# A decode step (gated attention plus GLU): written engine order, and wo split by heads around the last V pair

## The chip, the cores and the metric

One core of a Trainium2 chip. The metric is the device time of one execution in microseconds (us), lower is better. Each set of runs was made on one chip, and sets fell on different chips. The kernel before ran in the rounds of each set, but set 3 was compared with the eleven executions of before from set 2 (same chip) and only two new ones. An execution is called fast when it lies within 1.5% of the fastest of its kernel in the set, slow otherwise. "Span" is the time from the first to the last instruction of a profiled execution.

## The reference, cut to what matters

```python
g = sigmoid((x * gate_w).sum())                       # one number
q = x @ wq                                            # 32 heads of 128
k, v = last W = 4096 rows of the caches, 8 kv heads   # 4 query heads each
a = softmax(q k^T / sqrt(128)) v   @ wo               # wo: 4096 x 512
b = (sigmoid(x @ w_gate) * (x @ w_up)) @ w_down       # 512 -> 1792 -> 512
out = g * a + (1 - g) * b                             # 512 numbers, one token
```

One token, so each weight and each cache row is used once: 30.7 MB are read, in this order of use: wq 4.2 MB, K 8.4, w_gate and w_up 3.7, V 8.4, w_down 1.8, wo 4.2.

## The kernel before

The K and V caches come in four pairs of kv heads (2.1 MB each). VectorE transposes each K half pair (kT), TensorE forms scores S, a softmax over all heads follows, then PV, then a head selection (o_ps), a small transpose (oX, oY), and the products with wo row block by row block (`add_row`: two matmuls of 128x256 for a block of 128 rows). The GLU branch adds its 14 row blocks of w_down to the same sum a_ps. The engines' order is left to a scheduler, which may move instructions within what their data allow.

```python
# loads, all on one queue, in this order
wq; K0..K3; w_gate; w_up (7/8 at once, the last 1/8 in four loads "wx" of 32 rows)
V0, V1, V2; V3 first half; w_down[0:7]; V3 second half; w_down[7:14]
wo in pieces of 8, 8, 8, 5, 2, 1 row blocks                   # waits for wq's buffer
...
S_ps = ps_S.tile([P, 4, 512], F32)                            # scores of all, one tile
for v in range(2):                                            # softmax
    nc.scalar.activation(e_sb[:, v], S_ps[...], AF.Exp, ...)
    nc.vector.transpose(eT[...], e_sb[:, v])                  # L242
...
nc.vector.tensor_scalar_add(sge, sge, 1.0)                    # GLU's gate
nc.vector.reciprocal(sg, sge)                                 # L266
nc.vector.scalar_tensor_tensor(h_sb, gu_ps[1], gg[:, 1:2], sg, ...)   # L268
nc.vector.transpose(hT, h_sb)                                 # L273
...
for a in range(4):                                            # PV, L304
    for m in range(16):
        if a == 3 and m == 8: down(0, 7)
        nc.tensor.matmul(pv_ps[32*a:32*a+32], lhsT=eT[:, a, 4*m:4*m+4], rhs=vv[a][:, 4*m:4*m+4], ...)
nc.scalar.copy(pv_sb, pv_ps)                                  # all heads at once
down(7, 10); o_ps (4 matmuls); oT; down(10, 12); oX; oY_ps; oY; down(12, 14)
for c in range(32):                                           # wo behind everything
    add_row(oY[:, c:c+1], wo_sb[:, c], ...)                   # L290
res; store
```

## Time and profile before

| | before |
|---|---|
| time, median of the first set | 84.41 us (84.08 to 84.76, 4 runs) |
| time, median of all 35 runs of the later sets | 83.8 us (82.85 to 85.02) |
| profiled execution | 83.79 us, span 81.6 us |
| loads end (the DMA engines' busy share falls to 0.07) | 75.2 us, the last packet at 75.5 |
| scores | 27.6 to 44.1 us |
| PV begins | 57.8 us |
| last matmul ends | 78.87 us |

How to read it: what a change can win is what lies between the end of the loads and the end of the span. The lines that this rests on are in the prediction.

### The profile page before, as it was taken

To read this page: it belongs to the slowest core of one execution; us is meant where nothing else is said; L and a number is where in the kernel's file an instruction comes from. 1 tells how busy PE (TensorE), PEld (TensorE's weight loads), DVE (VectorE), ACT (ScalarE), POOL (GpSimd) and SP (SyncE) were. 2 spreads that over 40 slices of the span, in tenths; PEclk is the share of its full clock that TensorE was granted. 3 is DMA by queue.
4 is the path that set the end of the run, shared out by engine and by line. 5 is a ranking of instruction groups with operands and counts; after the bars stand their busy time and mean duration, and the time that the engine had idled before them with its cause. 6 is when DMAs were issued, how large, how long until landed. Compare 5 with 4: busy or idle time off the path is not lost.

```text
span 81.6 us, 791 instructions
## 1 busy us (share of the span) xinstructions
PE 51.6 (63%) x313; PEld 24.0 (29%) x313; DVE 38.6 (47%) x50; ACT 10.1 (12%) x18; POOL 3.3 (4%) x10
## 2 busy tenths in 40 slices
PE   0200286999400499999999063300999999967960
PEld 0200122344000233444443033000433444545830
DVE  0601820034999999999903995699300000002020
ACT  2300000376500000000000200910000000020010
POOL 7800000000000000000000000000000000000000
PEclk9999999999998555999999997555555999999999
DMA  5969969999999999999999999999999999995000
GB/s 161 353 289 482 514 273 490 393 418 474 401 426 458 410 434 425 436 422 412 421 422 458 410 426 450 409 426 391 417 428 420 420 422 422 424 399 217 0 0 1
DMA packets 3050, 30.71 MB, mean 376 GB/s; under 512 B 356, under 2 KB 616, under 8 KB 1128
## 3 DMA queue, kind: packets, MB, share of 16 engines
q1 hardware_dynamic: 3042, 30.67, 89.7%
q8 instruction: 2, 0.03, 0.2%
q10 hardware_dynamic: 6, 0.00, 0.0%
HBM read 30.67 MB, written 0.00 MB: 376 GB/s over the span
## 4 chain that ended last, share of the span: by engine, by line
PE 55%; DVE 24%; DMA 15%; ACT 1%; issue 1%
PE S_ps L215 20%; PE pv_ps L304 17%; DMA wq_sb<-in_A_wq_dram 15%; PE q_ps L184 8%; PE a_ps L290 6%; DVE kT L209 5%; DVE sg L266 4%; DVE pm L222 3%; DVE eT L242 3%; DVE h_sb L268 3%; DVE qbig L197 2%; DVE qtT L189 2%; PE o_ps L313 1%; PE gu_ps L255 1%; DVE hT L273 1%
## 5 line engine op out<-in xcount | busy, mean ns | idle before, releaser
L215 PE MATMUL S_ps<-kT,qbig 128*128 128x512 bf16 x64 | 16.6, 424 | 6.2 <-DVE qbig L197 6.2
L209 DVE STREAM_TRANSPOSE kT<-kn 128x2048 f32<-128x2048 f32 x8 | 17.8, 2275 | 0.0
L304 PE MATMUL pv_ps<-vv,eT 128*32 128x512 bf16 x64 | 14.2, 436 | 0.0
L215 PEld LDWEIGHTS <-qbig 128*128 128x128 bf16 x64 | 6.7, 106 | 16.1 <-DVE qbig L197 7.0
L184 PE MATMUL q_ps<-wq_sb,xT 128*128 128x512 bf16 x32 | 8.4, 428 | 1.0 <-DMA wq_sb<-in_A_wq_dram 1.0
L304 PEld LDWEIGHTS <-eT 128*32 128x32 bf16 x64 | 5.8, 109 | 7.6 <-issue 3.6
L315 DVE TENSOR_TENSOR oT<-o_ps,rb 128x32 bf16<-128x32 f32 x1 | 0.2, 191 | 15.2 <-PE o_ps L313 15.2
L189 DVE STREAM_TRANSPOSE qtT<-q_sb 128x512 f32<-128x512 f32 x4 | 2.8, 702 | 7.5 <-ACT q_sb L186 7.5
L203 PE MATMUL S_ps<-ident,other 2*128 2x512 bf16 x4 | 2.0, 611 | 5.8 <-DVE other L141 5.8
L186 ACT CAST q_sb<-q_ps 128x512 bf16<-128x512 f32 x8 | 4.7, 585 | 6.5 <-PE q_ps L184 6.5
L184 PEld LDWEIGHTS <-xT 128*128 128x128 bf16 x32 | 3.4, 108 | 6.4 <-issue 3.7
L279 PE MATMUL rb_ps<-lsel,ones_f 128*128 128x32 f32 x2 | 0.6, 398 | 5.6 <-DVE lsel L277 5.6
L222 DVE TENSOR_REDUCE pm<-S_ps 128x1 f32<-128x1024 f32 x2 | 2.4, 1219 | 3.2 <-PE S_ps L215 3.2
L290 PE MATMUL a_ps<-wo_sb,oY 128*1 128x256 bf16 x64 | 3.7, 272 | 0.0
L263 ACT ACTIVATE sge<-gu_ps 128x448 f32<-128x448 f32 x1 | 0.5, 543 | 23.1 <-PE gu_ps L258 23.1
L290 PEld LDWEIGHTS <-oY 128*1 128x1 bf16 x64 | 2.8, 84 | 0.7
L266 DVE RECIPROCAL sg<-sge 128x448 f32<-128x448 f32 x1 | 3.0, 2954 | 0.0
L309 ACT COPY pv_sb<-pv_ps 128x512 f32<-128x512 f32 x1 | 0.6, 586 | 18.7 <-PE pv_ps L304 18.7
L268 DVE SCALAR_TENSOR_TENSOR h_sb<-gu_ps,gg,sg 128x448 bf16<-128x448 f32 x1 | 2.2, 2154 | 1.5 <-PE gu_ps L255 1.5
L166 DVE TENSOR_TENSOR gpr<-xr 1x512 f32<-1x512 bf16 x1 | 0.7, 679 | 4.6 <-DMA xr<-in_gate_w_dram 4.6
L149 PE MATMUL xt_ps<-ident,xr 1*128 1x1 bf16 x4 | 0.3, 166 | 3.5 <-POOL ident L130 3.5
L203 PEld LDWEIGHTS <-other 2*128 2x128 bf16 x4 | 0.6, 158 | 6.2 <-DVE other L141 5.9
(60 smaller groups left out, 32.5 us busy)
## 6 DMA issues: line engine op xcount, KB each, us to landing
kn<-in_A_k_cache_dram SPq DMA_DIRECT2D x4, 2048.0 KB, 27.2
vv<-in_A_v_cache_dram SPq DMA_DIRECT2D x3, 2048.0 KB, 19.1
wq_sb<-in_A_wq_dram SPq DMA_DIRECT2D x1, 4096.0 KB
wo_sb<-in_A_wo_dram SPq DMA_DIRECT2D x3, 1024.0 KB, 22.9
vv<-in_A_v_cache_dram SPq DMA_DIRECT2D x2, 1024.0 KB
wg_sb<-in_B_w_gate_dram SPq DMA_DIRECT2D x1, 1792.0 KB, 32.9
wd_sb<-in_B_w_down_dram SPq DMA_DIRECT2D x2, 896.0 KB
wu_sb<-in_B_w_up_dram SPq DMA_DIRECT2D x1, 1568.0 KB
```

Of the source, the lines that this page charges most:

```text
L184: nc.tensor.matmul(q_ps[:], lhsT=xT[:, c:c + 1].to_broadcast([P, P]), rhs=wq_sb[:, c, ks], start=(c == 0), stop=(c == DC - 1))
L186: nc.scalar.copy(q_sb[:, ks], q_ps[:])
L189: nc.vector.transpose(qtT[:].bitcast(F32)[:, kq], q_sb[:].bitcast(F32)[:, kq])
L203: nc.tensor.matmul(S_ps[:, u, :], lhsT=other[:].rearrange("p o y u -> p (o y u)"), rhs=ident[0:2, 0:2].rearrange("p (o y) -> p o y", o=1). ...
L209: nc.vector.transpose(kT[:].bitcast(F32), kn[a][:, v * KB:(v + 1) * KB, :] .rearrange("p n d -> p (n d)").bitcast(F32))
L215: nc.tensor.matmul(S_ps[:, 2 * v + hb, :], lhsT=q_st[:, a, dhi, :, t], rhs=k_v[:, hb * 16:(hb + 1) * 16, dhi, :, t], start=False, stop=(a ...
L222: nc.vector.tensor_reduce(pm2[:, v:v + 1], S_ps[:, 2 * v:2 * v + 2, :].rearrange("p a b -> p (a b)"), axis=AX.X, op=ALU.max)
L242: nc.vector.transpose(eT[:, :, v * KB:(v + 1) * KB, :].rearrange("p a n r -> p n a r"), e_sb[:, v, :].rearrange("p (n a r) -> p n a r", a= ...
L266: nc.vector.reciprocal(sg[:], sge[:])
L268: nc.vector.scalar_tensor_tensor(h_sb[:].rearrange("p j i -> p i j"), gu_ps[1][:, 0:FQ].rearrange("p (i j) -> p i j", j=NJ), gg[:, 1:2], s ...
L290: nc.tensor.matmul(a_ps[32 * i:32 * i + 1, i, 0:HN], lhsT=lhsT, rhs=rhs[:, i * HN:(i + 1) * HN], start=start, stop=stop)
L304: nc.tensor.matmul(pv_ps[32 * a:32 * a + 32, :, :], lhsT=eT[:, a, 4 * m:4 * m + 4, :].rearrange("p n r -> p (n r)"), rhs=vv[a][:, 4 * m:4 ...
```

## The change

Four things at once. Its intent: nothing but the last pieces of the last load shall remain to do once the stream of loads is over.

1. From the query projection on, TensorE, VectorE and ScalarE run in the order in which the program is written (`manual_schedule`), and that order puts GLU's vector work behind the exponentials' transposes and the first K transpose between the query's.
2. S becomes two tiles (one for each half v), so that the first maximum needn't wait for the second half; PV takes one of their PSUM buffers and a_ps the other.
3. Heads in two halves: the first half's selection, transpose and wo rows run while V3 is awaited. wo is stored by halves of heads, one loaded before V3, one after.
4. w_down moves to the end, in pieces of 8, 3, 2 and 1 row blocks.

```diff
+    WD_SPLIT = (0, 8, 11, 13, 14)
+    ORDERED = {PE, DVE, Activation}
-    ps_S = tile_pool(name="ps_S", bufs=1, space=PSUM)
+    ps_S = tile_pool(name="ps_S", bufs=2, space=PSUM)
 ... loads
-            load_pair(vv[3], A_v_cache, 3, 0, NP // 2)
-            dq.dma_start(wd_sb[:, 0:7], wd_v[:, 0:7])
-            load_pair(vv[3], A_v_cache, 3, NP // 2, NP)
-            dq.dma_start(wd_sb[:, 7:14], wd_v[:, 7:14])
-    for c0, c1 in zip(WO_SPLIT[:-1], WO_SPLIT[1:]):
-        dq.dma_start(wo_sb[:, c0:c1, :], wo_v[:, c0:c1, :])
+            dq.dma_start(wo_sb[:, 0], wo_v[0])
+            load_pair(vv[3], A_v_cache, 3, 0, NP // 2)
+            load_pair(vv[3], A_v_cache, 3, NP // 2, NP)
+            dq.dma_start(wo_sb[:, 1], wo_v[1])
+    for j0, j1 in zip(WD_SPLIT[:-1], WD_SPLIT[1:]):
+        dq.dma_start(wd_sb[:, j0:j1, :], wd_v[:, j0:j1, :])
 ... front
+    ctx.enter_context(tc.manual_schedule(engines=ORDERED))
+        if k == 1: kTs[0, 0] = k_transpose(0, 0)          # in the query loop
+            copy = nc.scalar.copy if qd == 3 else nc.vector.tensor_copy   # 2 of 8 qbig copies
 ... GLU's sge, sg, h_sb, hT now written behind eT, rs, lsel
 ... tail
+    pv(0)
+    (rb_ps matmul, rb)
+    pv(1); pv_copy(0); pv(2)
+    heads_out(0); heads_rows(0)
+    pv(3); pv_copy(1)
+    out_rows(0, 0, 8);  heads_out(1)
+    out_rows(0, 8, 16); heads_rows(1)
+    out_rows(1, 0, 16)
+    for j in range(NJ): add_row(hT[:, j, 0:1], wd_sb[:, j, :], False, j == NJ - 1)
```

## The prediction

> **What bounds the kernel now.** I read the page's slices first, then the waits of the DMA queue, then the chain of work that ended last, then the timeline of the softmax stage and of the tail.
>
> The slices (2.04 us each; the busy tenths of TensorE, VectorE, the granted clock and the DMA engines):
>
> ```profile
> PE   0200286999400499999999063300999999967960
> DVE  0601820034999999999903995699300000002020
> PEclk9999999999998555999999997555555999999999
> DMA  5969969999999999999999999999999999995000
> ```
>
> The DMA row stands at 9 from slice 6 to 35. So the 30.7 MB of inputs arrive without a break, at about 0.42 MB per us, until 75 us, and the kernel can't end before that. But the span is 81.6 us: for the last three slices nothing is loaded and TensorE works alone. That tail is what can be won. The PE row has two holes, near 23 us and from 45 to 57 us, and after each the clock row says 5: half clock.
>
> When each load lands can be read from the SyncE queue, whose issues each wait for the load eight places before:
>
> ```profile
> 46.74 0.33 SPq L124 DMA_DIRECT2D wo_sb<-in_A_wo_dram  x1
> 51.63 0.33 SPq L124 DMA_DIRECT2D wo_sb<-in_A_wo_dram  x1
> 56.54 2.80 SPq L124 DMA_DIRECT2D wo_sb<-in_A_wo_dram  x2
> 61.20 0.33 SPq L124 DMA_DIRECT2D wo_sb<-in_A_wo_dram  x1
> ```
>
> The releasers are V0, V1 and V2, and at the last line the first w_down half: the V pairs of 2.1 MB land at 46.74, 51.63 and 56.54 us, one each 4.9 us, so 0.426 MB/us. After 61.20 us 6.16 MB are still to come; at this rate they end at 75.7 us. The row of DMA by stretches agrees: full rate to 74 us, half rate to 75.2, nothing after.
>
> The end of the chain:
>
> ```profile
> 54.58 2.25 DVE eT L242 x2
> ...
> 57.91 11.63 PE pv_ps L304 x52
> ...
> 70.20 1.83 PE pv_ps L304 x8
> 72.03 0.02 issue
> 72.05 0.59 ACT pv_sb L309
> 72.65 0.04 issue
> 72.69 1.09 PE o_ps L313 x8
> ...
> 74.47 4.40 PE a_ps L290 x78
> 78.87 0.40 DVE res L330
> ```
>
> The whole attention output must pass eviction, head selection and a transpose before the first wo row may be multiplied, and all 64 wo matmuls (of the 78) come after it, although most of wo lay there long before. PV itself begins at 57.9 us, 11 us after V0 landed, because the exponentials' transposes stand behind the GLU on VectorE:
>
> ```profile
> 46.85 2.95 DVE L266 RECIPROCAL sg<-sge 128x448 f32<-128x448 f32 x1
> 51.75 2.15 DVE L268 SCALAR_TENSOR_TENSOR h_sb<-gu_ps,gg,sg 128x448 bf16<-128x448 f32 x1 [1.53 <-PE gu_ps L255]
> 53.94 0.65 DVE L273 STREAM_TRANSPOSE hT<-h_sb 128x448 bf16<-128x448 bf16 x1
> 54.51 2.33 DVE L242 STREAM_TRANSPOSE eT<-e_sb 128x1024 bf16<-128x1024 bf16 x2
> ```
>
> **What the Trainium skill says.** "TensorE: Matmul & The Clock Gate", Part 1, says that the clock is 1.2 or 2.4 GHz, set by activity in free-running windows of 3413 ns. The trace agrees on the windows: the clock falls at 25.96 and 49.85 us and rises at 32.8 and 63.5 us, all whole multiples of 3.41 us apart, and 512-column matmuls stand 427 ns apart before such a rise and 215 ns after. The page speaks of an idle window; here the window 46.44 to 49.85 us had 1.43 us of matmuls and the clock still fell, while 1.97 us in the window before it kept the clock. So I put the threshold at about half a window. "DMA: Bandwidth & Descriptors", Where 436 GB/s comes from, gives a fabric ceiling of 435 GB/s; the 426 measured here lie close to it, so I expect no order of loads to end the stream sooner. The same page, Anatomy of one DMA, says that completion follows the last byte by a write receipt; the 0.4 us between the last busy DMA (75.2) and my 75.7 is my allowance.
>
> **The change part by part.**
>
> Start of the scores. Before, VectorE did the first two K transposes and the last query transpose in such an order that the eight qbig copies ended at 27.6. Now the first K transpose follows the first query transpose: kn0 lands at 17.8 (the third wx issue, which waits for it), so it takes 17.8 to 20.1 (2.27 us), the query transposes go on to 22.65 (the last cast ends at 21.95, plus 0.7), six copies stay on VectorE (6 of 8 of 1.77, 1.3 us), two go beside them to ScalarE. Scores begin at about 24.0 instead of 27.56. Then seven transposes follow at 2.21 us (13.28 for 6), to 39.4; TensorE needs only 8 x 0.215 = 1.72 us for each, and ends about 41.3 instead of 44.1: 2.8 us earlier.
>
> Softmax. The first maximum (1.2 us) now runs before the last scores end, as S is two tiles. From 41.3: maximum 1.2, to 42.55; pm and mt to 43.15; from there the old durations of hm, mb, nb and exp (49.72 to 52.20) give the first eT at 45.7, two of 1.15, to 48.0. The 2.95 + 2.15 + 0.65 + 0.38 = 6.1 us of GLU are now behind it and end at about 54.5, where nobody waits. PV can begin at 47 to 48 instead of 57.8. This is ten us, but **it is not worth ten us**: V0 has only just landed (46.74). PV is from now on paced by the loads.
>
> Loads. The same bytes in another order after V2 (56.54): first half of wo 61.5, V3 in halves 63.9 and 66.4, second half of wo 71.3, w_down's 8, 3, 2 and 1 blocks 73.7, 74.7, 75.3 and about 75.7 us (estimates: bytes over 0.426). V3 lands 2.6 us later than now, but the work behind it shrinks. The buffers allow the order: wo takes the one that wq left at 21 us; the queue's eight places are never empty.
>
> TensorE from there, at full clock: pv(2) 56.6 to 60.1; first half's heads 1.1 for o_ps, 0.45 on VectorE, 0.3 for oY, to 62; pv(3) from 63.9 in two parts of 8 x 0.215, ends 68.3; ScalarE copy 0.6; 16 of the first half's 32 row matmuls beside it (16 x 0.0565 = 0.9; rate from 78 in 4.40); o_ps 69.0 to 70.1; oT and oX 0.45 with the other 16 rows beside; oY at 71.5. That is just when the second half of wo lands (71.3). Its 32 rows take 1.8, to 73.4; then the w_down rows follow their pieces; after the last piece (75.7) 2 matmuls remain, with latency 0.35: **76.05 us against 78.87**. The end (res, the store, 2.75 us from 78.87 to 81.6) doesn't change. Gain 2.8 us: about 81.7 us.
>
> Added: four matmuls for two oY (one before), two evictions of 64 rows for one of 128, some 0.6 us more of small work, all under a load's wait except the second half's, which is in the sum.
>
> **Rivals.**
>
> 1. The clock falls in front of V3. Between 61.95 and 63.9 us TensorE has nothing to do, and little between 65.65 and 66.35. A window that ends between about 63.3 and 65.6 us holds 0.85 to 1.5 us of matmuls, as little as the one at 46.44 or less. For it: that is two thirds of all positions of the free-running window. Against: the page wants an idle window, and one full window (3.4 us) of half-clock matmuls raises it again, as at 63.5 in the trace. Cost, worked for three positions: falling at 64.5, pv(3) ends at 69.0 and nothing is lost, since oY (71.9) then wants only 0.6 us more and the rows catch up before the last piece; falling at 63.5 without the next window counting, or at 65.4, pv(3) ends near 70, oY comes at 73.7 to 74.1, and 60 rows of 0.0565 follow: 77.3 to 77.5. Time 82.9 to 83.1 us, a gain of only 1.6 to 1.9%.
>
> 2. The load stream hides nothing more, and all of the gain is lost: the tail at half clock throughout. 60 rows at 0.113 instead of 0.0565 cost 3.4 us more, TensorE ends at 79, no gain: 84.5 us. Against: the rows kept the clock in the trace before from 70 to 79 us. I give it 5%.
>
> 3. The small last pieces (1 to 3 KB runs) stretch the stream. The stream before ended in pieces of the same kind (5, 2 and 1 KB runs) and had half rate for its last 1.2 us, so I count the same once more. If it were 1 us longer: 82.7 us.
>
> 4. The early gain counts in full (PV 10 us sooner, end at 72 us). The loads speak against it: not before 75.7.
>
> **Range and chances.** Half for the case bound by loads (81.7), four tenths for the clock's fall (81.9 to 83.1), one tenth for something unseen. Executions before spread over 0.7 us. My number is 82.1 us, range 81.2 to 83.4. The line of 2% faster is 82.8 us: the load case lies a full 1 us beyond it, about half of the clock cases lie beyond it. Faster 0.68, same 0.30, slower 0.02.
>
> **What would show it.** Right: scores begin near 24 and end near 41.3; PV begins between 46.8 and 48.5; GLU's reciprocal after eT; TensorE's waits in front of pv for V, not for eT; V3 landing at 66.4; the last w_down matmul at 76 us within 0.5 us of its load; span 78.8. The clock row with a 5 near 64 to 70 us would be rival 1: then oY comes after 73 us, and the w_down rows don't wait. Wrong: a DMA row with gaps after slice 13, a last landing later than 76.3, or a new wait on VectorE (rb or oT behind the GLU after 60 us).

## The result, and the profile after

The first set gave 80.98 us (80.8 to 81.74, 4 runs) against 84.41 (84.08 to 84.76): ratio 0.961, 95% interval 0.954 to 0.968. Ratios here are the mean time of one kernel's fast runs over that of the other's in the same rounds, so not quite the ratio of the medians quoted; as far as I can reproduce them, the profiled executions of the later sets are left out. Faster, as forecast, but 80.98 lies below the range of 81.2 to 83.4.

The slices of the kernel after (2.0 us each), TensorE, VectorE, granted clock and DMA:

```profile
PE   0200193999914788998887557999789579998940
...
DVE  0600820029859999999986349999300200001020
PEclk9999999999999999999999995699999985899997
DMA  3979998999999999999999999999999999999600
```

The DMA row has no gap, as before, and now TensorE works until just behind it: the idle hole of TensorE from 45 to 57 us is gone, and the tail of three slices without loads is down to two. The chain that ended last, in order of time, is no longer TensorE's (in the kernel before, S, PV and the rows of a_ps were 43% of it) but the stream's:

```profile
32.68 18.96 DMA vv<-in_A_v_cache_dram
51.64 0.02 issue
51.66 24.14 DMA wd_sb<-in_B_w_down_dram
75.79 0.04 issue
75.84 0.65 PE a_ps L306 x6
76.48 0.40 DVE res L366
```

VectorE's timeline in the softmax stage shows the new order, eT ahead of GLU:

```profile
46.73 2.37 DVE L280 STREAM_TRANSPOSE eT<-e_sb 128x1024 bf16<-128x1024 bf16 x2 [1.91 <-ACT e_sb L278]
...
49.75 2.95 DVE L290 RECIPROCAL sg<-sge 128x448 f32<-128x448 f32 x1
52.82 2.17 DVE L292 SCALAR_TENSOR_TENSOR h_sb<-gu_ps,gg,sg 128x448 bf16<-128x448 f32 x1
```

TensorE's timeline at the end (start, duration, line, what; in brackets the idle time before and what ended it):

```profile
63.96 4.65 PE L319 MATMUL pv_ps<-vv,eT 128*32 128x512 bf16 x13 [0.90 <-DMA vv<-in_A_v_cache_dram]
...
72.50 1.91 PE L306 MATMUL a_ps<-wo_sb,oY 128*1 128x256 bf16 x32 [0.27 <-DVE oY L339]
74.25 1.41 PE L306 MATMUL a_ps<-wd_sb,hT 128*1 128x256 bf16 x22
75.84 0.60 PE L306 MATMUL a_ps<-wd_sb,hT 128*1 128x256 bf16 x6 [0.18 <-DMA wd_sb<-in_B_w_down_dram]
```

| | predicted, load case | profile after |
|---|---|---|
| scores begin, end | 24.0, 41.3 | 24.8, 42.25 |
| PV begins | 47 to 48 | 48.03 |
| V3's first half | 63.9 | 63.96 |
| second oY ready | 71.5 | 72.44 |
| last piece of w_down lands | 75.7 | 75.79 |
| last matmul ends | 76.05 | 76.48 |
| span | 78.8 | 79.3 |

Every step of the load case stands within 1 us, and the three that follow a load (PV, V3, the last landing) within 0.1; and the predicted 81.7 us of that case is still 0.7 too long. So the error is not in the mechanism.

This profile is one of five of the kernel after, and they do not all end in the same way. In three (this one, e13, e14b) the last rows wait for the last piece of w_down. In the other two (e7 at 80.58 us, e14a at 80.75) they don't wait: the chain that ended last runs from V3's first half through pv(3), which the clock's fall had slowed, and through 60 rows without a pause. From e7's:

```profile
63.95 5.20 PE pv_ps L319 x16
...
72.50 3.62 PE a_ps L306 x60
76.12 0.40 DVE res L366
```

The last matmul ended at 76.11 to 76.48 us in the first three and at 76.12 and 76.29 in the other two. So load stream and TensorE end almost together here, and which of them is last changes from one execution to the next.

Before saying where the error is, the parts have to be told apart, and the size of the gain settled.

### The profile page after: what moved, and what is told of

It reads as the page before. It is cut to its first block, busy times and chain, and to the rows that moved or that the text cites. A ratio compares the mean times of both kernels' runs of the same rounds, so it can differ in the third digit from the quotient of the medians.

```text
span 79.3 us, 825 instructions
## 1 busy us (share of the span) xinstructions
PE 55.5 (70%) x324; PEld 25.5 (32%) x324; DVE 39.1 (49%) x51; ACT 11.4 (14%) x21; POOL 3.7 (5%) x13
## 2 busy tenths in 40 slices
DMA packets 2762, 30.71 MB, mean 387 GB/s; under 512 B 324, under 2 KB 584, under 8 KB 840
## 3 DMA queue, kind: packets, MB, share of 16 engines
q1 hardware_dynamic: 2754, 30.67, 92.0%
HBM read 30.67 MB, written 0.00 MB: 387 GB/s over the span
## 4 chain that ended last, share of the span: by engine, by line
DMA 91%; SPq 3%; PE 1%; DVE 1%; issue 0%
DMA kn<-in_A_k_cache_dram 37%; DMA wd_sb<-in_B_w_down_dram 30%; DMA vv<-in_A_v_cache_dram 24%; SPq L85 2%; PE a_ps L306 1%; SPq L81 1%; DVE res L366 1%
## 5 line engine op out<-in xcount | busy, mean ns | idle before, releaser
L319 PE MATMUL pv_ps<-vv,eT 128*32 128x512 bf16 x64 | 17.6, 439 | 3.0 <-DVE eT L280 1.4
L235 PE MATMUL S_ps<-kT,qbig 128*128 128x512 bf16 x64 | 15.2, 377 | 5.0 <-DVE qbig L224 2.8
L319 PEld LDWEIGHTS <-eT 128*32 128x32 bf16 x64 | 6.8, 109 | 12.9 <-issue 6.2
L235 PEld LDWEIGHTS <-qbig 128*128 128x128 bf16 x64 | 6.1, 97 | 14.1 <-issue 4.2
L208 PE MATMUL q_ps<-wq_sb,xT 128*128 128x512 bf16 x32 | 8.9, 448 | 1.4 <-DMA wq_sb<-in_A_wq_dram 1.4
L306 PE MATMUL a_ps<-wo_sb,oY 128*1 128x256 bf16 x64 | 4.8, 272 | 0.3 <-DVE oY L339 0.3
L325 ACT COPY pv_sb<-pv_ps 64x512 f32<-64x512 f32 x2 | 1.2, 579 | 20.9 <-PE pv_ps L319 20.9
L280 DVE STREAM_TRANSPOSE eT<-e_sb 128x1024 bf16<-128x1024 bf16 x2 | 2.4, 1224 | 1.9 <-ACT e_sb L278 1.9
```

Source lines behind the costliest of these rows:

```text
L208: nc.tensor.matmul(q_ps[:], lhsT=xT[:, c:c + 1].to_broadcast([P, P]), rhs=wq_sb[:, c, ks], start=(c == 0), stop=(c == DC - 1))
L235: nc.tensor.matmul(S_ps[v][:, hb, :], lhsT=q_st[:, a, dhi, :, t], rhs=k_v[:, hb * 16:(hb + 1) * 16, dhi, :, t], start=False, stop=(a == HP ...
L280: nc.vector.transpose(eT[:, :, v * KB:(v + 1) * KB, :].rearrange("p a n r -> p n a r"), e_sb[:, v, :].rearrange("p (n a r) -> p n a r", a= ...
L306: nc.tensor.matmul(a_ps[32 * i:32 * i + 1, i, 0:HN], lhsT=lhsT, rhs=rhs[:, i * HN:(i + 1) * HN], start=start, stop=stop)
L319: nc.tensor.matmul(pv_ps[32 * (a % 2):32 * (a % 2) + 32, a // 2, :], lhsT=eT[:, a, 4 * m:4 * m + 4, :].rearrange("p n r -> p (n r)"), rhs= ...
```

## The experiments

Five sets in all with the first. Sets 2, 3 and 5 ran on one chip (median of before 83.55, 83.55 and 83.78), set 4 on another (83.91). 95% intervals of the ratios are ±0.003 to ±0.007.

| run | set | median us | ratio to before |
|---|---|---|---|
| e1 before again | 2 | 83.67 | 1.008 |
| e3 order, with the old loads and tail | 2 | 82.44 | 0.990 |
| e6 after, GLU's vector work first | 2 | 82.90 | 0.992 |
| e5 after, late scores | 2 | 81.08 | 0.975 |
| e7 after again | 3 | 81.72 | 0.980 |
| e2 after without any written order | 3 | 89.27 | 1.072 |
| e4 after, w_down in one piece | 3 | 82.44 | 0.988 |
| e9 after, wo's first half behind V3 | 3 | 80.82 | 0.971 |
| e8 after, V3 wait filled | 4 | 80.88 | 0.966 |
| e10 e9 with a wait filled | 4 | 81.39 | 0.973 |
| e11 e6 with TensorE kept busy | 4 | 81.76 | 0.974 |
| e12 after, only TensorE's order written | 4 | 82.01 | 0.980 |
| e13 after, third set | 5 | 80.81 | 0.968 |
| e15 after, w_up loaded whole | 5 | 81.34 | 0.975 |

All outputs are right.

### e1: the kernel before, again

No edit.

> The kernel before, unchanged, to see what my sum started from. The profile of before was an execution of 83.79 us with a span of 81.6, while the median is 84.4; the profile of after was 80.94 with 79.3, close to its median. Theory A: the execution I had read was a quick one. Then spans of this kernel spread over 81.6 to 82.5 with time minus span about 2.2 in each, longer where the granted clock is lower, and the median span is about 82.2. Theory B: the span is 81.6 in nearly all runs, and the time outside the span varies. In both the ratio to before is 1.00.

The spans of its six executions were 81.0, 81.6, 81.7, 81.8, 82.3 and 82.7 with times 1.9 to 2.0 us longer: theory A's spread, though not its 2.2 us outside the span, and not with its clock, which was 0.87 to 0.90 in all. The two identical kernels differ by 0.8% here, so nothing under 1% is taken as an effect below by its ratio alone. The new profile (span 81.0) shows one reason for a spread: the clock rose during PV at 62.2 us instead of 63.5, and the last matmul ended at 78.27 instead of 78.87. TensorE sets this kernel's end, and so every shift of its clock window does too.

### e2 and e12: what the written order is worth

e2 removes it, e12 keeps it for TensorE alone.

```diff
e2:
-    ctx.enter_context(tc.manual_schedule(engines=ORDERED))
e12:
-    ORDERED = {PE, DVE, Activation}
+    ORDERED = {PE}
```

> The kernel after without the written order: the scheduler again orders the engines. By the instruction order it puts GLU's reciprocal (2.95 us) in front of the copy of the head maxima, but leaves GLU's product and transpose behind the exponentials. PV then begins near 50.5 instead of 48. Theory 'slack up to about 51' (as with the late scores, where PV began at 50.3 at no cost): 80.9 to 81.3, same as after. Theory 'the order is the gain': 82.5 or more.

> The kernel after with the written order for TensorE alone, VectorE and ScalarE left to the scheduler. By the instruction order VectorE then runs GLU's reciprocal in front of the copy of the head maxima and the second K transpose in front of the qbig copies; TensorE no longer waits for the denominators before PV and no longer has the wo rows in front of the last V pair, as it had with no written order (89.3 us). Theory 'TensorE's order is nearly all of the 8 us': PV begins near 52.9, 1.2 us later than in the kernel with GLU in front (82.9): 83 to 84 us. Theory 'VectorE's order is': 86 or more.

e2 took 89.27 us: some 8 us more than after and 5.7 more than before. My expectation had looked at VectorE's order only. The timeline of TensorE in e2 shows what I had overlooked:

```profile
56.36 0.61 PE L346 MATMUL rb_ps<-lsel,ones_f 128*128 128x32 f32 x2 [5.25 <-DVE lsel L284]
...
73.37 1.90 PE L305 MATMUL a_ps<-wo_sb,oY 128*1 128x256 bf16 x28
...
75.22 3.40 PE L318 MATMUL pv_ps<-vv,eT 128*32 128x512 bf16 x15
```

The denominators' matmul (rb_ps) stands in front of PV again, and TensorE waits in it until 56.4 for the sums of the exponentials, which PV doesn't need; and nearly all of the first half's wo rows (73.4) stand in front of nearly all of pv(3) (75.2), whose second heads then still have their whole chain to go. By the page's slices the loads were over at 75 us, 10 us before the last matmul. e12 took 82.01 us with VectorE's and ScalarE's order still the scheduler's: TensorE's order alone accounts for some 7 of the 8 us (7.3, between two sets). In its profile, which is of its slowest execution (83.01), PV began at 53.07 as expected (52.9), but the cost was 1 us less than expected.

### e6 and e11: GLU in front of the exponentials' transposes

```diff
e6: the lines sge, sg, h_sb, hT moved in front of
     for v in range(2): activation(e_sb ...); transpose(eT ...)
e11: e6, and
+    keep_warm(23)      # matmuls 128x512 of a loaded weight into a PSUM tile that nobody reads
     pv(0)
```

> The kernel after with one part undone: GLU's vector work (reciprocal, product, transpose, 6.1 us) written in front of the exponentials' transposes, as the kernel before ran it. PV then begins at about 52.2 instead of 48.0. Theory 'slack': TensorE then works through V0 to V2 without pauses and reaches V3 at 65 to 66 us, when it lands; time 80.8 to 81.3, no change. Theory 'the GLU position is the gain': 3 us or more of the 4 us come through, time 83 or above.

> The kernel with GLU's vector work in front of the exponentials' transposes (82.9 us), plus 23 such matmuls in TensorE's idle time before PV (23 x 0.2155 = 5.0 us of the 5.6). PV still begins at 51.7. Theory 'what the late PV costs is the half clock': PV runs at full clock from its start, saves 2.7 us, reaches V3 before it lands, and the time is that of after, 80.7 to 81.5. Theory 'the 4.3 us count as such': 82.5 or more, as without them.

In e6 PV began at 51.73 as expected, and the time was 82.90, 1.8 us above e5 of the same set (1.4 by the means of the fast runs). So "slack" failed in size: 1.8 of some 4 us come through. TensorE's timeline:

```profile
51.73 6.20 PE L319 MATMUL pv_ps<-vv,eT 128*32 128x512 bf16 x16 [5.62 <-DVE eT L292]
...
58.20 3.63 PE L319 MATMUL pv_ps<-vv,eT 128*32 128x512 bf16 x16
62.50 3.61 PE L319 MATMUL pv_ps<-vv,eT 128*32 128x512 bf16 x16 [0.67 <-ACT pv_sb L325]
```

The first pair takes 6.2 us, as 5.6 us of idling have halved the clock (3.6 at full clock, in e11; 5.1 in the kernel after, whose clock had fallen at 47.65 and rose again at 51.06). pv(3) begins at 67.8, where V3 is there in full from about 66.3 (e13), and the last matmul is at 78.1.

e11 fills the idle time with work for nobody. PV then began later (52.99) and still had its second oY at 73.3 instead of 74.6: PV ran at full clock throughout (0.977 granted in the mean of the span). So the half clock is at least 1.3 us of what e6 lost up to there. It isn't all: the kernel after had that oY at 72.4, and at 71.4 where its own clock stayed up from 52.3 on (e13), so a PV that begins some 5 us late costs 0.9 to 1.9 us at full clock too. The time of 81.76 lies between the two theories' numbers, because TensorE then had to wait for the last load until 76.65, 0.8 us later than in the profile after. What was happening there can be read from the busy times by stretches (the stretch, its length, busy time of TensorE, its weight loads, VectorE, ScalarE, GpSimd, granted clock, DMA share, GB/s):

```profile
75.00:75.50 0.50, 0.50 (x14) 0.43 (x10) 0.00 (x0) 0.00 (x0) 0.00 (x0) 1.00 0.13 47
75.50:76.00 0.50, 0.50 (x14) 0.38 (x12) 0.00 (x0) 0.00 (x0) 0.00 (x0) 1.00 0.08 29
76.00:76.50 0.50, 0.46 (x10) 0.22 (x6) 0.00 (x0) 0.00 (x0) 0.00 (x0) 1.00 0.05 16
```

A share of 0.13 of sixteen engines is two of them, 0.08 one: one or two DMA engines were still at work when the others had long finished. e6's profile has the same lag (a share of 0.08 from 76.0 to 76.5), but TensorE was later still there and hid it.

### e5: the front undone

```diff
-        if k == 1:
-            kTs[0, 0] = k_transpose(0, 0)
-            copy = nc.scalar.copy if qd == 3 else nc.vector.tensor_copy
+            nc.vector.tensor_copy(q_dst[...], q_src[...])
```

> The kernel after with the front undone: the first K transpose behind the query's, all eight qbig copies on VectorE. Scores begin near 27.5 instead of 24.8 and end at 44.7 instead of 42.3, PV begins near 50.5. Theory 'slack': PV is paced by V anyway, time 80.8 to 81.3, no change. Theory 'every microsecond in front counts': 83.4.

PV began at 50.31 instead of 48.03, and the time was 81.08 (four of six at 80.93 to 81.10, two at 82.1 and 82.2). That is at most 0.3 us above the quick executions of after (80.57 to 81.02), in other sets: PV waits for the V pairs anyway, and 2.3 us are within the slack. With e6 the edge can be bracketed: PV at 50.3 is nearly free, at 51.7 with a cold clock it costs 1.4 to 1.8 us more.

### e3: the order alone

After's order and front, before's loads and tail (wo last in six pieces, all heads in one go; PV in a buffer of the S tiles).

> The written order and the front of the kernel after (early first K transpose, S in two tiles, GLU's vector work behind the exponentials' transposes), with the loads and the tail of the kernel before: wo last in pieces of 8, 8, 8, 5, 2, 1, all heads in one go. Theory 'order is enough': PV begins at 48, ends near 67, oY is there near 70, and the wo rows follow their pieces, the last of which lands at 75.7; the last matmul at 76 to 76.5, time 81.0, as after. Theory 'the load order is needed': the rows after oY are the bound, the last matmul at 77.5 or later, time 82 to 82.6.

82.44 us: 1.1 us below before, 1.4 above e5 of the same set. PV began at 47.39, and oY was there at 68.55, so the order does what it should. But then the rows come in bursts, one for each piece of wo, with waits between:

```profile
71.07 1.04 PE L305 MATMUL a_ps<-wo_sb,oY 128*1 128x256 bf16 x16 [1.43 <-DMA wo_sb<-in_A_wo_dram]
73.57 3.47 PE L305 MATMUL a_ps<-wo_sb,oY 128*1 128x256 bf16 x32 [1.46 <-DMA wo_sb<-in_A_wo_dram]
```

The last 32 rows take 3.47 us instead of the 1.91 that 32 rows take in the kernel after, and the clock row of its page stands at 5 and 6 there. So the second theory holds, by way of the clock: with wo last the rows behind the last pieces run cold, the last matmul is at 77.06. The order of loads and the halves are worth some 1.4 us, the written order and front some 1.1 by the medians, in this set; the latter is 0.8 by fast runs (ratio 0.990), at the edge of what e1 lets pass as an effect.

### e9 and e10: wo's first half behind V3

```diff
e9:
-            dq.dma_start(wo_sb[:, 0], wo_v[0])
             load_pair(vv[a], A_v_cache, a, 0, NP // 2)
             load_pair(vv[a], A_v_cache, a, NP // 2, NP)
+            dq.dma_start(wo_sb[:, 0], wo_v[0])
             dq.dma_start(wo_sb[:, 1], wo_v[1])
e10: e9, and keep_warm(6) between heads_rows(1) and out_rows(1)
```

> The kernel after with the first half of wo loaded behind the last V pair instead of in front of it. V3 lands at 61.5 instead of 66.4, PV ends near 63.7, the second heads are ready near 67, then the rows follow wo's halves (66.4 and 71.3) and w_down. Theory 'the stream's end is the bound': no change, 80.9 to 81.4. Rival 'TensorE in waits of over 1.5 us goes cold, and cold rows take 0.11 us each': the rows behind 71.3 run at half clock, the last matmul at 77 or later, 0.6 to 1.2 us slower than after.

> The kernel with wo behind V, plus 6 such matmuls in the wait for wo's second half. In the profile of wo behind V the clock fell at 71.5, and 32 rows took 3.36 us instead of 1.8. Theory 'clock': with the wait filled the rows end near 73.5, the w_down rows wait for their pieces, the last matmul at 76.2 instead of 76.7; 80.3 to 80.7. Rival 'the last landing is the bound and cold rows hide behind it': no change, 80.7 to 81.0.

e9 took 80.82 us, as after in its quick executions. Its rows were cold as the rival said (32 rows in 3.53 us from 71.64), yet that cost little: the last matmul ended at 76.70, in after at 76.48. e10 warmed them (1.91 us from 71.75), TensorE then waited 0.62 and 0.17 us for w_down, and nothing was won: 80.74 to 81.02 in three executions, 81.8 to 82.0 in the other three. So loading half of wo in front of the last V pair, which the change does, is not needed for the gain; with the written order, splitting the heads' work and w_down at the end suffice. Which of these two does more, no run separates, and S in two tiles was not tested alone either.

### e4: w_down in one piece

```diff
-    WD_SPLIT = (0, 8, 11, 13, 14)
+    WD_SPLIT = (0, 14)
```

> The kernel after with w_down loaded in one piece instead of 8, 3, 2 and 1 blocks. Theory 'the end hangs on the last load': all 28 w_down rows (28 x 0.057 = 1.6 us) come after the last landing instead of 6 (0.6 with latency), so the last matmul is 0.9 to 1.2 us later, time 82.0 to 82.2; if the clock falls in the wait before them, up to 1.5 us more. Rival 'the small pieces themselves stretch the stream': the half rate of the stream's last 1.8 us shrinks, landing at 75.0, and the cost is under 0.5 us.

82.44 us. Both kernels fall in a quicker and a slower group in this set, so like must be compared with like: the three quick executions of e4 are at 81.87 to 82.03, the two of e7 at 80.58 and 80.84, which is 1.25 us; the slower ones (82.85 to 83.41, and 81.65 to 81.97) differ by 1.4. In its profile the w_down rows began at 75.89, all 28 behind the landing, against 75.84 for the last 6 in after. So the single piece lands no sooner than the last small one: the small pieces don't stretch the stream (rival 3 of the prediction), and they save about what 22 rows less behind the landing should, 22 x 0.057 = 1.2 us.

### e7, e8, e13, e14: the size of the gain, and a second group

```diff
e8:
     heads_rows(0)
+    keep_warm(5)
     pv(3)
```

> The kernel after, unchanged, against before in rounds of one chip. The first result compared four executions of each (80.98 and 84.41 us). Theory 'the gain is the tail, and some of the 3.4 us are the chip and the few executions': ratio 0.970 to 0.976, before near 83.6, after near 81.0 to 81.2. Theory 'the first figure was the true one': ratio 0.957 to 0.965.

> The kernel after with 5 matmuls of 128x512 whose result nobody reads, in TensorE's wait for V3 (5 x 0.2155 = 1.08 us, between the first heads and pv(3)). The result stays right. Theory 'rival 1, the clock': the executions of after fall in two groups, 80.6 to 81.1 and 81.65 to 82.0, because a window of the clock that ends at a bad place takes pv(3) and the rows to half clock. With the wait filled the second group disappears: all 80.5 to 81.1, median near 80.8. Theory 'the groups come from elsewhere, such as the load stream': both groups remain.

> The kernel after, a third set. Two groups again: near 80.8 and near 81.8. Theory 'the first figure was three quick executions out of four against slow ones of before': ratio 0.965 to 0.980.

> One more profile of the kernel after. If it is of the slower group (over 81.5 us): theory 'lagging DMA engine': TensorE waits for the last w_down piece until 76.5 or later, and one or two DMA engines are busy after 75.5. Rival 1 'clock': the w_down rows don't wait, oY comes after 73, the last matmul at 77.3 or later with the loads in by 75.8.

> Again one more profile of the kernel after, with the same two theories as the look before: in the slower group either a wait for the last w_down piece until 76.5 or later (lagging DMA engine), or rows that don't wait and a late oY, after 73 (clock).

e7 gave 80.58, 80.84, 81.65, 81.80, 81.82 and 81.97: ratio 0.980. e13, the same kernel on the same chip, gave 80.71 to 80.93 in all six: 0.968; the two looks gave 80.75 and 80.57. With the first set, 13 of 18 executions of this kernel are at 80.57 to 81.02 and five at 81.65 to 81.97. e8, with the wait filled, gave 80.70 to 80.98 in all six, which rival 1 had called for, but e13 did so with nothing filled, so e8 doesn't show that the second group was the clock. In the profiles of the kernel after the clock's fall cost nothing: in the first one it fell at 64.7 us, in pv(3), in e13 it did not and the second half of wo was waited for (0.40 us at 71.6), and both executions ended alike (80.94 and 80.84).

No profile of this very kernel fell in the second group. The one profile of a close relative that did (e11, 81.76) shows lagging DMA engines, not a slow TensorE. The granted clock doesn't set the groups apart: e7's slower executions have 0.936 to 0.957, e13's quick ones 0.935 to 0.957; that speaks against the clock, though a mean doesn't say where it fell. That the second group of after is lagging engines is likely, not shown.

### e15: how the loads fall on the DMA engines

```diff
-    dq.dma_start(wu_sb[... 0:LM], ...)                    # 7/8 of w_up
-    for h in range(2): for b in range(2): dq.dma_start(wx_sb[32*b:32*b+32, h, :], wx_v[h, b])
+    dq.dma_start(wu_sb[:], B_w_up.rearrange("(p c) f -> p c f", c=DC))
     (and GLU's four wx matmuls become two ordinary ones)
```

> The kernel after with w_up loaded whole, 128 rows in one load, instead of seven eighths of it in that way and the last eighth through four loads of 32 rows each; the same bytes. These four loads seem to be there to move bytes from some DMA engines to others. Theory 'the end hangs on the slowest DMA engine': the stream's uneven end grows, the last landing comes 0.5 to 1.5 us later, time 81.3 to 82.5. Rival 'the engines even out by themselves': no change, or up to 0.3 us quicker as four loads and six matmuls fall away.

81.34 us against 80.81: 0.5 us slower, with the same bytes in fewer loads. That is under 1%, but the six executions of each don't overlap (81.25 to 81.70 and 80.71 to 80.93), and the profile shows where it comes from. The stretches of its last microseconds, and after them those of e13:

```profile
74.50:75.00 0.50, 0.48 (x12) 0.24 (x8) 0.00 (x0) 0.00 (x0) 0.00 (x0) 1.00 0.13 51
...
75.50:76.00 0.50, 0.50 (x12) 0.34 (x7) 0.00 (x0) 0.00 (x0) 0.00 (x0) 1.00 0.13 45
```

```profile
74.50:75.00 0.50, 0.50 (x12) 0.38 (x9) 0.00 (x0) 0.00 (x0) 0.00 (x0) 1.00 0.46 162
75.00:75.50 0.50, 0.50 (x10) 0.26 (x6) 0.00 (x0) 0.00 (x0) 0.00 (x0) 1.00 0.09 33
```

In e15 all but two of the sixteen DMA engines are done by 74.5 us and two (0.13) go on to 76. In e13 about half of them go on to 75, and the two are done by some 75.5 (0.09). So where the kernel after waits for its last load, as in e13, its end is the end of its two slowest DMA engines. The Trainium skill, "DMA: Bandwidth & Descriptors", Why a DMA increments its semaphore by 16 and not by 1, says that a load uses as many engines, up to 16, as divide the slowest dimension on both sides, and the lowest-numbered ones. The four small loads' slowest source dimension is 8, so by this page they use eight engines and take 0.23 MB / 2 / 8 = 14.3 KB from each of the other eight; at 426 / 16 = 26.6 KB per us that is an estimate of 0.54 us. Measured were 0.53. It fits, if the two slow engines are among the other eight; which ones they are, no run here shows. If they were the two that the last section's page calls usually slower (7 and 15), only 15 would be among them, so that this explanation stays open.

A further move of bytes would probably gain little: the other engines end at 75.0 in e13. I found no version clearly better than the kernel after.

## Why the prediction was wrong, point by point

**The mechanism: right.** The end was to pass from TensorE to the load stream, and did; the table above has the steps. "Not worth ten us" was right: e5 shows 2.3 us of PV's lead to be worth 0.3 us at most.

**The range: wrong**, by the step "Gain 2.8 us: about 81.7 us", and then by "four tenths for the clock's fall". The first subtracts a difference of spans, read from one execution, from a median time. In the first set, the one that was forecast:

| term | us |
|---|---|
| median of before | 84.41 |
| span, 81.6 to 79.3 (predicted to 78.8) | -2.3 |
| time outside the span, 2.19 to 1.64 (no term for it) | -0.55 |
| the execution of before that I read (83.79) was that much quicker than the median; that of after (80.94) was not | -0.58 |
| median of after | 80.98 |

So of the 3.43 us between the medians the span, all that the sum was about, is 2.3, and 1.13 us come from two terms that the sum took as zero. Its 2.8 us of span were 0.5 too many; the omitted terms outweigh that, and the time fell below the range. That the executions of before in that set lay above the median of all later ones is chance.

- The time outside the span was 2.05 us in the mean over 35 executions of before (1.94 over the six of e1, the same kernel), 1.66 over after's (e7, e13). I had taken it as constant. It isn't one: 2.01 in e2, 1.96 in e12, 2.21 in e3, 1.80 in e5, 1.65 in e4, e6 and e9. It goes neither with the loads alone (e2 and e12 have after's) nor with the written order alone (e3 has it). What it is, the profiles don't show; this stays open.
- The sample: before spreads over 2 us (82.85 to 85.02), and three executions on one chip gave 84.48 where the later 35 give 83.8. I saw that the profiled execution, 83.79, lay below all three and drew nothing from it. Set against 83.8, the quick executions of after gain 3.0 us (e13 and its set), of which 2.5 are span (81.6 to 79.15, medians); by fast runs alone the gain of that set is 2.7 us.
- **Rival 1 was over-weighted.** The clock did fall where it said (64.7 us), and oY came at 72.4, 0.9 later than in the sum (in e13, where it did not fall, at 71.4, as in the sum). But the rows caught up at 0.057 us each before the last piece landed at 75.8, in that execution with 0.18 us to spare. In e7 and e14a nothing was left to spare (see above), but their last matmul was no later. The clock fell in front of or in pv(3) in four of the five profiles of this kernel, at 63.2 to 64.9 us, and cost nothing that can be seen (e8 against e13: 80.88 and 80.81). The sum for a fall at 64.5 had said so; the costly positions, 65.4 or a following window that doesn't count, came up in no profile. The 0.4 us that rival 1 added to my number, and the 83.4 at the top of the range, had no ground in these runs.
- In the other direction, the last matmul ended 0.4 us later than predicted: the pieces of 2 and 1 blocks landed together, so that 6 matmuls (0.60 us) and not 2 came behind the last landing.
- A wait that I had not foreseen: pv(2) waits 0.67 us for ScalarE's eviction of the first half (the bracket in e6's lines, and the same in after). It lies in the slack.
- Slips in the working, each worth 0.1 us or less: 2.1 MB in 4.9 us are 0.428 MB/us and not 0.426; 75.7 less 75.2 is 0.5 and not 0.4; and DMA engines were still busy after 75.2 (a share of 0.07 to 75.6). The section on the anatomy of a DMA describes the software path, while these loads use the hardware queue; in the profile after, the last landing (75.79) followed the last packet (75.69) by 0.1 us. The threshold of half a window for the clock's fall fits the profile of before, but not the later ones (last section).

**Rival 2** (rows at half clock throughout) did not happen in after; in e3 and e9, where TensorE waits for wo's pieces, it happened to 32 rows. **Rival 3** (small pieces stretch the stream) was refuted by e4. **Rival 4** (all ten us count) did not happen: the span became 2.3 us shorter.

**What the prediction had no word on** is the largest effect: without the written order the same loads and the same tail take 89.3 us. My reading is that splitting the heads gave the scheduler new freedom on TensorE, and that it used it to put waiting work in front of ready work; e12 shows that TensorE's order is what matters, not why the scheduler chose as it did.

The size of the gain remains a range: ratios 0.961, 0.980 and 0.968 in three sets. The middle one has four executions of the slower group, and e7's executions without the profiled one (80.58, its quickest) reproduce it; by the fast executions listed for e7, that one included, it would be 0.972.

## What to carry to other kernels

When every byte is read once, first find the end of the load stream, then ask what is still to do behind the last byte, and arrange the rest so that this is as little as possible: the last operand needed should be one whose product needs nothing else (here w_down's rows), in shrinking pieces. Making an early stage faster is worth nothing once it waits for loads, but letting it start so late that TensorE goes cold adds to the cost of the delay (at least 1.3 us at the second oY, e6 against e11). When a difference of spans is turned into a time, check first that the profiled execution lies at the kernel's median, and that time minus span is the same for both kernels.

## What the Trainium skill lacked or had wrong

- "TensorE: Matmul & The Clock Gate", Part 1, speaks of an idle window (3.41 us) before the clock falls. Here it fell after windows with 1.43 us (before, 46.44 to 49.85) and 1.95 us (after, 61.3 to 64.7) of matmuls: a window need not be idle. How little work suffices, the summed matmul time doesn't say: the clock stayed after 1.71 us (after, 20.3 to 23.8) and fell after 2.39 (e2, 66.2 to 69.6).
- The same page says that one busy window raises it. Windows with 2.79 us (before, 56.68 to 60.09) and 3.03 us of matmuls (e2, 56.0 to 59.4) did not, the full ones after them did; but one with 2.64 us did (e14b, 63.2 to 66.6).
- "DMA: Bandwidth & Descriptors", Latency and other measured facts, says which DMA engines are usually slower (7 and 15), and has a best guess at the cause, called uncertain, that is tied to the software descriptor queue; here 30.67 of 30.71 MB went over the hardware queue and two engines still lagged. It has no number for what this costs at the end of a stream. Here two of sixteen engines ended 1.5 us behind the others (e15), 0.5 with bytes moved away from eight of them (e13), over a stream of 30.7 MB; and in the profiles of e6 and e11 one or two of them nearly another microsecond later.
- No page says that the time outside the span, from the first to the last instruction, differs between kernels: 1.6 to 2.2 us here in the means of the kernels (2.8 in one execution of e11), differing by up to 0.6 us between kernels of the same order (e3 and after) and 0.3 between kernels of the same loads (e2 and after).
